# Weight staging, a PSUM bank for half-made weights, and one attention's exponentials and low parts moved between engines

## The chip, the cores and the metric

The kernel runs on one core of a Trainium2 chip. The metric is the device time of one execution in microseconds, the median of several runs. TensorE is called PE here, VectorE DVE, ScalarE ACT, GpSimd POOL and SyncE SP.

## The reference

A windowed attention is followed by two feed-forward networks on its output. Batch 4, 8 heads, 576 positions, head size 64; 2304 tokens, model width 512, inner width 2048.

```python
scores = scale * np.matmul(q, k.transpose(0, 1, 3, 2))
rel = pos[:, None] - pos[None, :]
mask_plain = (rel >= 0) & (rel < window)                                  # heads 0 to 3
mask_dil = (rel >= 0) & (rel < window * dilation) & (rel % dilation == 0)  # heads 4 to 7
scores = np.where(masks[None, :, :, :], scores, -1000000000.0)
attn = np.exp(scores - np.max(scores, axis=-1, keepdims=True))
attn = attn / (np.sum(attn, axis=-1, keepdims=True) + 1e-09)
x = np.matmul(attn, v)                  # then 2304 x 512
h = x @ w_in                            # first network
x = (np.maximum(h, 0.0) + alpha * np.minimum(h, 0.0)) @ w_out
h = x @ w_in2                           # second network
g = np.where(h >= 1, h, np.where(h <= -1, 0.0, (h + 1) ** 2 / 4.0))
out = g @ w_out2
```

## The kernel before

**The networks.** Activations stand in SBUF as X, 512 features on 4 x 128 partitions, 2304 tokens in the free dimension. Each network goes over five token tiles (512 wide, one of 256), and each tile over 16 slots, one for each 128 of the inner width: 160 slots in all. A product of fp32 numbers is made of three matmuls on a high and a low part of each operand. So `f_h` (L316) issues 12 matmuls of 512 columns into one bank of `ps_h`, which has two banks, and `f_y` (L355) issues 12 into the four banks of y. Between them `f_g` (L330) applies the nonlinearity: in the first network ACT makes relu(−h) into g (L339), the DVE makes h + alpha' g in place in the PSUM bank (L341), ACT copies that to gh (L347), and `f_cut` has the DVE make gl = h_ps − gh (L353), the last reader of the bank. PE's order is `f_h` of slot k, then `f_y` of slot k − 2. The low parts of the weights, wil (L288) and wol (L313), are made by POOL from a high part that ACT copied (L287, L312).

**The weights.** They arrive as 64-bit numbers. A weight piece (128 x 512) is loaded by SP into a staging buffer st (L248, 512 KB). Three operations of the DVE turn it into fp32: L276, L277 and L271. The first two are a mask and a shift of the upper word into wf or wo, each later one reads st and the half-made piece, both in SBUF. `conv(k)` issues k such operations; 5 or 6 come in each slot of tile 0, two of them ahead of L341 and one ahead of gl. There are five staging buffers for the first five pieces, three of which exist only at the beginning; later pieces have two. `more()` issues a load whenever a piece is done. In tile 4 and the next one the second network's weights are made in the same way.

**The attention.** It comes in 24 groups of 3 x 128 query rows, six for each batch. The six of batch 0 run at the beginning, with banks of their own; those of batches 1 to 3 are threaded through the first three tiles. There are two attention points in each slot, one after `f_h` and one after `f_y`, and a new group starts at every fifth point: `start` (scores, maximum, exponentials), then `a_turn` three points later (transposes, a copy to pT), `a_values` after five, `a_out` after eight (`STAGES`, L56). Each takes a bank of `ps_a`, which has two buffers used in turn. In batch 1 the mask is added on PE (L122), the maximum is read from PSUM (L136), and six exponentials of ACT read the scores from PSUM with the maximum as a bias (L143). Slots 0 and 1 have their `f_h` issued ahead of the slot loop (lines 466 to 485), so that between the start of group 7 and `f_h` of slot 2 PE has attention work alone.

**Order.** The kernel is scheduled by hand: each engine executes in the order in which the code issues, and waits at the first instruction that isn't ready. SP's queue is in order too. alpha and most of the mask are loaded from POOL's queue (L399, L400).

Of the kernel before, what the change touches and what calls it, by code (L numbers as in the profile page):

```python
# [10 lines left out]
F32 = mybir.dt.float32  # L11
# [11 lines left out]
P = 128  # L23
# [15 lines left out]
QK = KW + QW  # L39

NE = 8
EST = (2, 3, 4)
SCALE = 1.0 / math.sqrt(D)
NEG = -1.0e30
TILES = (
# [7 lines left out]
EARLY = (5, 6)  # L53
BEFORE = ((2, 1), (1, 3))

STAGES = (3, 5, 8)  # L56


def _subs(sb):
# [12 lines left out]
def attention_then_two_ffns(ctx: ExitStack, tc: tile.TileContext, a0, aqk, av, w1i, w1o, w2i, w2o, alpha, masks, ident, out):  # L72
# [6 lines left out]
    s_p = ctx.enter_context(tc.tile_pool(name="s_p", bufs=1))  # L79
    st_p = ctx.enter_context(tc.tile_pool(name="st_p", bufs=3))  # L80
    ps_h = ctx.enter_context(tc.tile_pool(name="ps_h", bufs=2, space=bass.MemoryType.PSUM))
    ps_a = ctx.enter_context(tc.tile_pool(name="ps_a", bufs=2, space=bass.MemoryType.PSUM))

    X = [const.tile([P, NT], F32, name=f"X{c}") for c in range(NC)]
    al = const.tile([P, NF], F32, name="al")
# [157 lines left out]

    def w_load(ph, f, part):
        w = ((w1i, w1o), (w2i, w2o))[ph][part]
        own = ph == 0 and pieces(0).index((ph, f, part)) in EST
        st = (sp if own else cv_p).tile([P, DM, 2], I32, tag="sx" if own else "st", name="st", bufs=len(EST) if own else 2)
        nc.sync.dma_start(st.rearrange("p a b -> p (a b)"), w[f].bitcast(I32))  # L248
        cv[ph, f, part] = st

    def w_make(ph, f, part):


        st = cv.pop((ph, f, part))
        top, low = st[:, :, 1], st[:, :, 0]
        if part:
            wf = w_pool(f).tile([P, DM], F32, tag=f"o{f}", name="wo")
            wo[ph, f] = wf
        else:
            hi = w_pool(f).tile([P, DM], F32R, tag=f"ih{f}", name="wih")  # L260
            lo = w_pool(f).tile([P, DM], F32R, tag=f"il{f}", name="wil")
            if ph == 0 and f in (1, 3):

                wf = sp.tile([P, DM], F32, tag="wx", name="wf")
            else:
                wf = cv_p.tile([P, DM], F32, tag="wf", name="wf", bufs=1)
            wt[ph, f] = (hi, lo)
        wi = wf.bitcast(I32)

        def last():  # L270
            nc.vector.scalar_tensor_tensor(wi, low, 29, wi, ALU.logical_shift_right, ALU.bitwise_or)  # L271
            if not part:
                cut.append((wf, hi, lo))

        return [
            lambda: nc.vector.tensor_scalar(wi, top, 0x07FFFFFF, 3, ALU.bitwise_and, ALU.logical_shift_left),  # L276
            lambda: nc.vector.scalar_tensor_tensor(wi, top, -0x40000000, wi, ALU.bitwise_and, ALU.bitwise_or),  # L277
            last,
        ]

# [22 lines left out]
    def wo_split(n, f):  # L303
        wf = wo[n[0], f]
        if (n, f) == slots[-1]:

            hi = cv_p.tile([P, DM], F32R, tag="wf", name="woh", bufs=1)
            lo = cv_p.tile([P, DM], F32R, tag="st", name="wol")
# [21 lines left out]
    def f_g(n, f, between):  # L330
        ph, t = n
        w = TILES[ph][t][1]
        ps = ht.pop((n, f))[:, :w]
        t = g_p.tile([P, TW], F32, tag="g", name="g", bufs=1)[:, :w]
        hi = g_p.tile([P, TW], F32R, tag="gh", name="gh")[:, :w]
        lo = g_p.tile([P, TW], F32R, tag="gl", name="gl")[:, :w]
        if ph == 0:

            nc.scalar.activation(t, ps, AF.Relu, scale=-1.0)  # L339
            between()  # L340
            nc.vector.scalar_tensor_tensor(ps, t, al[:, f:f + 1], ps, ALU.mult, ALU.add)  # L341
        else:
            nc.vector.tensor_scalar(t, ps, 1.0, -1.0, ALU.min, ALU.max)  # L343
            nc.scalar.activation(t, t, AF.Square, bias=half, scale=0.5)  # L344
            between()
            nc.vector.tensor_tensor(ps, ps, t, ALU.max)  # L346
        nc.scalar.activation(hi, ps, AF.Copy)  # L347
        gt[n, f] = (hi, lo)
        return ps

    def f_cut(n, f, ps):
        hi, lo = gt[n, f]
        nc.vector.tensor_tensor(lo, ps, hi.bitcast(F32), ALU.subtract)  # L353
# [33 lines left out]
    with tc.manual_schedule(), ExitStack() as late:  # L387
# [8 lines left out]
        warm = sp.tile([P, TW], BF16, tag="warm", name="warm")  # L396
        nc.scalar.dma_start(idt, ident)
        nc.scalar.dma_start(mask[:, :2 * GS], masks[:, :2 * GS])
        nc.gpsimd.dma_start(al, alpha)  # L399
        nc.gpsimd.dma_start(mask[:, 2 * GS:], masks[:, 2 * GS:])  # L400
        nc.vector.memset(warm, 0.0)
        nc.vector.memset(half, 0.5)
        pend_l = pieces(0)
# [2 lines left out]
        for i in range(NGB):  # L406
            a_load_qk(i)
            a_load_v(i)
            if i < 2 + len(EST):
                w_load(*pend_l.pop(0))  # L410
        nc.scalar.activation(half, half, AF.Exp, scale=0.0)
        nc.scalar.activation(half, half, AF.Copy, scale=0.5)
        for i in range(2):
# [84 lines left out]
        def attention_point():  # L498
# [4 lines left out]
                nxt += 1  # L503
            for i in list(at):
                k = point - at[i]
                if k == STAGES[0]:
                    a_turn(i, ps_a, "a")
                elif k == STAGES[1]:
                    a_values(i, ps_a, "a")
# [140 lines left out]
```

## Time and profile before

| | |
|---|---|
| median of 3 runs | 903.1 us (902.39 to 905.37) |
| the profiled execution | 902.28 us, of which the span is 900.5 us |
| PE busy | 875.4 us, 97% |
| DVE busy | 498.9 us, 55% |
| ACT busy | 372.3 us, 41% |
| POOL busy | 267.0 us, 30% |
| mean granted clock of PE | 0.981 of full |

A time in the trace counts from the start of the span. The busy shares are averages over stages with different limits, so the stretches are to be read one by one: the attention of batch 0 up to about 42 us, tile 0 with the making of the first network's weights up to about 146 us, tiles 1 to 3 up to 400 us, tile 4 and the first tile of the second network up to about 560 us, with weights again, and then matmuls alone.

### The profile page before, as it was taken

The page shows a single profiled execution, that of the slowest core. Times are in us where ns is not written, and L with a number is a line of the kernel's source. Part 1 is how long each engine was busy: PE and PEld are TensorE (multiplying, and loading weights), DVE is VectorE, ACT ScalarE, POOL GpSimd, SP SyncE. Part 2 cuts the span into 40 slices and gives each one's busy share as a digit, 9 for nine tenths or more (in the row PEclk, how much of TensorE's full clock was granted, in tenths as well). Part 3 has the DMA queues.
Part 4 walks back from the last instruction along what each step waited for, and adds up shares of the span by engine and source line. Part 5 has one row for each costly group of instructions (what it writes and reads, how often), then busy time and mean ns, then how long its engine had stood idle before and what let it go on. Part 6 is the DMA issues. An engine that isn't in the chain of part 4 may idle for free.

```text
span 900.5 us, 13858 instructions
## 1 busy us (share of the span) xinstructions
PE 875.4 (97%) x5470; PEld 720.6 (80%) x5470; DVE 498.9 (55%) x785; ACT 372.3 (41%) x745; POOL 267.0 (30%) x208
## 2 busy tenths in 40 slices
PE   7879899999999999999999999999999999999998
PEld 4568677888888888998888877888888888888898
DVE  6779897433353333346998896543354335433443
ACT  3434344534345334444334443433343334333454
POOL 3323331221212122444443343222222222222243
PEclk6789999999999999999999999999999999999999
DMA  9477463112112200001443331010001000100100
GB/s 360 140 197 211 138 189 106 38 41 71 38 41 71 65 1 1 1 2 47 138 133 104 118 125 39 1 47 1 0 1 48 1 0 1 47 1 0 44 5 24
DMA packets 24640, 59.34 MB, mean 66 GB/s; under 512 B 2752, under 2 KB 10448, under 8 KB 24576
## 3 DMA queue, kind: packets, MB, share of 16 engines
q1 hardware_dynamic: 24192, 58.09, 20.9%
q8 instruction: 43, 0.70, 0.3%
q14 instruction: 21, 0.17, 0.1%
q0 software_dynamic: 96, 0.20, 0.1%
q10 hardware_dynamic: 288, 0.16, 0.1%
HBM read 53.73 MB, written 4.72 MB: 65 GB/s over the span
## 4 chain that ended last, share of the span: by engine, by line
PE 81%; DVE 10%; DMA 4%; ACT 2%; issue 2%; SPq 0%; ACTq 0%; DVEq 0%
PE h_ps L326 13%; PE y L365 13%; PE y L367 13%; PE y L366 13%; PE h_ps L328 13%; PE h_ps L327 13%; DMA st<-w1o 2%; DVE wo L277 1%; DVE wo L271 1%; DVE gl L353 1%; DMA st<-w1i 1%; PE s_ps L129 1%; DVE wf L277 1%; PE t_ps L191 1%; PE o_ps L202 1%
## 5 line engine op out<-in xcount | busy, mean ns | idle before, releaser
L313 POOL TENSOR_TENSOR wol<-wo,woh 128x512 fp32r<-128x512 f32 x160 | 213.7, 1336 | 513.3 <-ACT woh L312 509.2
L326 PE MATMUL h_ps<-xh,wil 128*128 128x512 f32 (+1 forms) x640 | 242.5, 379 | 8.9 <-DVE gl L353 8.8
L365 PE MATMUL y<-gh,wol 128*128 128x512 f32 (+1 forms) x640 | 238.9, 373 | 0.6 <-POOL wol L313 0.6
L328 PE MATMUL h_ps<-xh,wih 128*128 128x512 f32 (+1 forms) x640 | 238.3, 372 | 0.0
L327 PE MATMUL h_ps<-xl,wih 128*128 128x512 f32 (+1 forms) x640 | 237.4, 371 | 0.0
L367 PE MATMUL y<-gl,woh 128*128 128x512 f32 (+1 forms) x640 | 236.7, 370 | 0.0
L366 PE MATMUL y<-gh,woh 128*128 128x512 f32 (+1 forms) x640 | 235.9, 369 | 0.0
L347 ACT ACTIVATE gh<-h_ps 128x512 fp32r<-128x512 f32 (+1 forms) x160 | 88.9, 556 | 212.5 <-PE y L366 97.5
L353 DVE TENSOR_TENSOR gl<-h_ps,gh 128x512 fp32r<-128x512 f32 (+1 forms) x160 | 102.0, 638 | 120.4 <-ACT gh L347 111.4
L326 PEld LDWEIGHTS h_ps<-xh,wil 128*128 128x128 f32 x640 | 121.2, 189 | 34.7 <-DVE gl L353 13.1
L328 PEld LDWEIGHTS h_ps<-xh,wih 128*128 128x128 f32 x640 | 121.2, 189 | 22.9
L365 PEld LDWEIGHTS y<-gh,wol 128*128 128x128 f32 x640 | 120.6, 188 | 22.8 <-issue 1.6
L327 PEld LDWEIGHTS h_ps<-xl,wih 128*128 128x128 f32 x640 | 121.4, 190 | 21.1 <-DVE xl L300 0.5
L367 PEld LDWEIGHTS y<-gl,woh 128*128 128x128 f32 x640 | 120.4, 188 | 21.9
L366 PEld LDWEIGHTS y<-gh,woh 128*128 128x128 f32 x640 | 120.5, 188 | 20.7
L344 ACT ACTIVATE g<-g,half 128x512 f32<-128x512 f32 (+1 forms) x80 | 54.5, 681 | 147.2 <-DVE g L343 147.0
L312 ACT ACTIVATE woh<-wo 128x512 fp32r<-128x512 f32 x160 | 99.6, 623 | 0.0
L341 DVE SCALAR_TENSOR_TENSOR h_ps<-g,al,h_ps 128x512 f32<-128x512 f32 (+1 forms) x80 | 55.9, 699 | 76.5 <-ACT g L339 75.9
L343 DVE TENSOR_SCALAR g<-h_ps 128x512 f32<-128x512 f32 (+1 forms) x80 | 50.8, 635 | 67.1 <-PE h_ps L328 66.8
L346 DVE TENSOR_TENSOR h_ps<-h_ps,g 128x512 f32<-128x512 f32 (+1 forms) x80 | 51.7, 646 | 60.5 <-ACT g L344 60.5
L288 POOL TENSOR_TENSOR wil<-wf,wih 128x512 fp32r<-128x512 f32 x32 | 44.6, 1394 | 110.4 <-ACT wih L287 106.0
L339 ACT ACTIVATE g<-h_ps 128x512 f32<-128x512 f32 (+1 forms) x80 | 44.2, 553 | 28.9 <-PE h_ps L328 28.8
(60 smaller groups left out, 513.8 us busy)
## 6 DMA issues: line engine op xcount, KB each, us to landing
st<-w1i SPq DMA_DIRECT2D x16, 512.0 KB, 4.1
st<-w1o SPq DMA_DIRECT2D x16, 512.0 KB, 3.8
st<-w2i SPq DMA_DIRECT2D x16, 512.0 KB, 3.2
st<-w2o SPq DMA_DIRECT2D x16, 512.0 KB, 3.3
qk<-aqk SPq DMA_DIRECT2D x36, 208.0 KB, 4.2
vz<-av SPq DMA_DIRECT2D x36, 195.0 KB, 4.2
out_t<-X SPq DMA_DIRECT2D x16, 256.0 KB, 2.0
e_in<-a SPq DMA_DIRECT2D x6, 416.0 KB, 8.8
```

The costliest lines, as they stand in the source:

```text
L312: nc.scalar.activation(hi, wf, AF.Copy)
L313: nc.gpsimd.tensor_tensor(lo, wf, hi.bitcast(F32), ALU.subtract)
L326: nc.tensor.matmul(ps[:, :w], wl[:, cs], xh[:, :w], start=(c == 0), stop=False)
L327: nc.tensor.matmul(ps[:, :w], wh[:, cs], xl[:, :w], start=False, stop=False)
L328: nc.tensor.matmul(ps[:, :w], wh[:, cs], xh[:, :w], start=False, stop=(c == NC - 1))
L341: nc.vector.scalar_tensor_tensor(ps, t, al[:, f:f + 1], ps, ALU.mult, ALU.add)
L344: nc.scalar.activation(t, t, AF.Square, bias=half, scale=0.5)
L347: nc.scalar.activation(hi, ps, AF.Copy)
L353: nc.vector.tensor_tensor(lo, ps, hi.bitcast(F32), ALU.subtract)
L365: nc.tensor.matmul(o, wl[:, cs], gh, start=(f == 0), stop=False)
L366: nc.tensor.matmul(o, wh[:, cs], gh, start=False, stop=False)
L367: nc.tensor.matmul(o, wh[:, cs], gl, start=False, stop=(f == NF - 1))
```

## The change

- All weight pieces go through five staging buffers `st` (NST) for the whole run; `more()` keeps up to five pieces loaded or in work. The room comes from a smaller descriptor scratch (`dynamic_dma_scratch_size`).
- From slot 0 on (`in_psum`) the first two operations of a piece write a PSUM bank, tag "w", and the third reads it and writes the piece to SBUF.
- `ps_a` has one buffer for tag "a" and one for tag "w" instead of two in turn. While pieces are being made, attention uses "a" alone; `bank()` alternates again when no pieces are left. In the first stage outputs use "w".
- Batch 1 subtracts the maximum with the DVE, from PSUM to SBUF, and one exponential of ACT follows.
- `STAGES` for batch 1 are 3, 4, 7 instead of 3, 5, 8.
- In the first network the DVE writes h + alpha' g to SBUF, into g, which has two buffers; gh and gl are made from there. In tile 0 POOL makes gl instead of the DVE.
- alpha and the rest of the mask are loaded from SP's queue behind the inputs of two groups.

```diff
-EST = (2, 3, 4)
+NST = 5
-STAGES = (3, 5, 8)
+STAGES = ((3, 4, 7), (3, 5, 8))
...
-    ps_a = ctx.enter_context(tc.tile_pool(name="ps_a", bufs=2, space=bass.MemoryType.PSUM))
+    ps_a = ctx.enter_context(tc.tile_pool(name="ps_a", bufs=1, space=bass.MemoryType.PSUM))
...
         src, s, mx = sc_t.pop(i)
+        if i < 2 * NGB:
+            nc.vector.tensor_tensor(s, src, mx[:, :, None].to_broadcast([P, 2 * GS, KEYS]), ALU.subtract)
+            nc.scalar.activation(s, s, AF.Exp, scale=SCALE)
+            s_t[i] = s
+            return
...
+        w0 = ps_a.tile([P, DM], F32, tag="w", name="w_ps").bitcast(I32) if in_psum else wi
...
-            nc.vector.scalar_tensor_tensor(wi, low, 29, wi, ALU.logical_shift_right, ALU.bitwise_or)
+            nc.vector.scalar_tensor_tensor(wi, low, 29, w0, ALU.logical_shift_right, ALU.bitwise_or)
...
-            lambda: nc.vector.tensor_scalar(wi, top, 0x07FFFFFF, 3, ALU.bitwise_and, ALU.logical_shift_left),
-            lambda: nc.vector.scalar_tensor_tensor(wi, top, -0x40000000, wi, ALU.bitwise_and, ALU.bitwise_or),
+            lambda: nc.vector.tensor_scalar(w0, top, 0x07FFFFFF, 3, ALU.bitwise_and, ALU.logical_shift_left),
+            lambda: nc.vector.scalar_tensor_tensor(w0, top, -0x40000000, w0, ALU.bitwise_and, ALU.bitwise_or),
...
-            nc.vector.scalar_tensor_tensor(ps, t, al[:, f:f + 1], ps, ALU.mult, ALU.add)
+            nc.vector.scalar_tensor_tensor(t, t, al[:, f:f + 1], ps, ALU.mult, ALU.add)
+            ps = t
...
-        nc.vector.tensor_tensor(lo, ps, hi.bitcast(F32), ALU.subtract)
+        (nc.gpsimd if n == order[0] else nc.vector).tensor_tensor(lo, ps, hi.bitcast(F32), ALU.subtract)
...
-        nc.gpsimd.dma_start(al, alpha)
-        nc.gpsimd.dma_start(mask[:, 2 * GS:], masks[:, 2 * GS:])
...
+            if i == 1:
+                nc.sync.dma_start(al, alpha)
+                nc.sync.dma_start(mask[:, 2 * GS:], masks[:, 2 * GS:])
...
-            while pend_l and sum(x[0] == 1 or pieces(0).index(x) not in EST for x in cv) < 2:
+            while pend_l and len(cv) + bool(todo) < NST:
                 w_load(*pend_l.pop(0))
...
+        def bank(i):
+
+            nonlocal turns
+            turns += not (todo or pend_w)
+            return "aw"[turns % 2]
```

PE's order where slots 0 and 1 begin. t_ps are the transposes of group 6, qk_88 the inputs of group 7, vz_89 the values of group 6, x_ps an output of the attention. Before:

```order
L191 MATMUL t_ps<-idt,s 128x128 x3
L122 LDWEIGHTS idt
L122 MATMUL s_ps<-mask,idt 32x384
...
L129 MATMUL s_ps<-qk_88 32x128 x12
L202 MATMUL o_ps<-vz_89,pT 32x130 x12
L326 MATMUL h_ps<-xh,wil 128x512
```

Now:

```order
L196 MATMUL t_ps<-idt,s 128x128 x3
L207 MATMUL o_ps<-vz_89,pT 32x130 x12
L122 LDWEIGHTS idt
L122 MATMUL s_ps<-mask,idt 32x384
...
L129 MATMUL s_ps<-qk_88 32x128 x12
L222 MATMUL x_ps<-idt,o 128x128 x3
L334 MATMUL h_ps<-xh,wil 128x512
```

The values of group 6 have moved ahead of the scores of group 7, and the output of group 6, which came after the twelve matmuls of slot 2, follows those scores directly.

The DVE's order at the same place, from the maximum of group 6 on. Before:

```order
L136 TENSOR_REDUCE mx<-s_ps 128x6
L141 TENSOR_SCALAR mx<-mx 128x6
L276 TENSOR_SCALAR wo<-st 128x512
L277 SCALAR_TENSOR_TENSOR wo<-st,wo 128x512
L271 SCALAR_TENSOR_TENSOR wo<-st,wo 128x512
L276 TENSOR_SCALAR wf<-st 128x512
L341 SCALAR_TENSOR_TENSOR h_ps<-g,al,h_ps 128x512
L277 SCALAR_TENSOR_TENSOR wf<-st,wf 128x512
L353 TENSOR_TENSOR gl<-h_ps,gh 128x512
L136 TENSOR_REDUCE mx<-s_ps 128x6
```

Now, from its subtraction on:

```order
L142 TENSOR_TENSOR s<-s_ps,mx 128x384
L284 TENSOR_SCALAR wo<-st 128x512
L285 SCALAR_TENSOR_TENSOR wo<-st,wo 128x512
L213 TENSOR_SCALAR rs<-o_ps 128x6
L214 RECIPROCAL rs<-rs 128x6
L215 TENSOR_TENSOR o<-o_ps,rs 128x384
L279 SCALAR_TENSOR_TENSOR wo<-st,wo 128x512
L284 TENSOR_SCALAR w_ps<-st 128x512
L349 SCALAR_TENSOR_TENSOR g<-g,al,h_ps 128x512
L285 SCALAR_TENSOR_TENSOR w_ps<-st,w_ps 128x512
L136 TENSOR_REDUCE mx<-s_ps 128x6
L142 TENSOR_TENSOR s<-s_ps,mx 128x384
```

The normalisation of group 6 (L213 to L215) now stands ahead of g of slot 0, gl is gone from this engine, and a subtraction stands behind each maximum.

SP's order of loads around the inputs of group 6 (qk_87) and of group 7 (qk_88). Before:

```order
L248 DMA st<-w1o 128x1024
L248 DMA st<-w1i 128x1024
L103 DMA qk_87<-aqk 64x832
L104 DMA qk_87<-aqk 64x832
L112 DMA vz_89<-av 64x3x260 x2
L248 DMA st<-w1o 128x1024
L248 DMA st<-w1i 128x1024
L103 DMA qk_88<-aqk 64x832
```

Now:

```order
L252 DMA st<-w1i 128x1024
L103 DMA qk_87<-aqk 64x832
L104 DMA qk_87<-aqk 64x832
L112 DMA vz_89<-av 64x3x260 x2
L252 DMA st<-w1o 128x1024
L252 DMA st<-w1i 128x1024
L252 DMA st<-w1o 128x1024
L103 DMA qk_88<-aqk 64x832
```

Two more pieces stand ahead of the first of these rows and one more between the inputs of the two groups; the piece next ahead of qk_88 waits in both for the DVE's last operation on an earlier piece.

## Rows read from the trace of the kernel before

**Rows 1.** Busy us of each engine by stretch, then clock, DMA share, GB/s

```profile
42.50:60.00 17.50, 11.37 (x89) 8.69 (x90) 12.06 (x20) 6.46 (x18) 4.77 (x4) 0.90 0.89 236
60.00:146.30 86.30, 81.60 (x572) 64.95 (x570) 79.02 (x114) 36.95 (x89) 30.57 (x22) 0.96 0.58 170
...
160.00:400.00 240.00, 240.00 (x1670) 202.07 (x1669) 89.44 (x169) 105.24 (x239) 59.81 (x46) 1.00 0.14 35
400.00:560.00 160.00, 158.52 (x712) 129.04 (x711) 134.81 (x180) 66.05 (x117) 63.85 (x47) 1.00 0.30 99
```

**Rows 2.** Waits of PE over the span: us in total, times, longest us

```profile
PE h_ps L326 <- DVE gl L353: 8.8, 8, 3.1
...
PE s_ps L129 <- DMA qk<-aqk: 2.9, 1, 2.9
...
PE y L365 <- POOL wol L313: 0.6, 1, 0.6
```

**Rows 3.** Groups of DVE instructions, 40 to 145 us: busy us, mean ns | idle before

```profile
L271 DVE SCALAR_TENSOR_TENSOR wo<-st,wo 128x512 int32<-128x512 int32 x14 | 16.3, 1162 | 0.3
L277 DVE SCALAR_TENSOR_TENSOR wo<-st,wo 128x512 int32<-128x512 int32 x14 | 14.8, 1054 | 0.3
L271 DVE SCALAR_TENSOR_TENSOR wf<-st,wf 128x512 int32<-128x512 int32 x12 | 10.5, 873 | 0.3
L341 DVE SCALAR_TENSOR_TENSOR h_ps<-g,al,h_ps 128x512 f32<-128x512 f32 x14 | 10.5, 748 | 0.0
L277 DVE SCALAR_TENSOR_TENSOR wf<-st,wf 128x512 int32<-128x512 int32 x12 | 10.4, 871 | 0.2
L353 DVE TENSOR_TENSOR gl<-h_ps,gh 128x512 fp32r<-128x512 f32 x13 | 9.0, 690 | 2.2 <-ACT gh L347 1.2
L276 DVE TENSOR_SCALAR wf<-st 128x512 int32<-128x512 int32 x11 | 7.9, 720 | 3.5 <-DMA st<-w1i 3.5
L276 DVE TENSOR_SCALAR wo<-st 128x512 int32<-128x512 int32 x14 | 7.0, 497 | 3.2 <-DMA st<-w1o 3.2
...
L136 DVE TENSOR_REDUCE mx<-s_ps 128x6 f32<-128x384 f32 x6 | 3.3, 550 | 0.9 <-PE s_ps L129 0.9
```

**Rows 4.** Timelines of DVE and POOL about 61 us: start, duration

```profile
60.75 0.69 DVE L277 SCALAR_TENSOR_TENSOR wo<-st,wo 128x512 int32<-128x512 int32 x1
61.47 1.67 DVE L271 SCALAR_TENSOR_TENSOR wo<-st,wo 128x512 int32<-128x512 int32 x1
...
61.12 1.47 POOL L288 TENSOR_TENSOR wil<-wf,wih 128x512 fp32r<-128x512 f32 x1 [3.27 <-ACT wih L287]
```

**Rows 5.** The largest group of POOL, 40 to 146 us

```profile
L313 POOL TENSOR_TENSOR wol<-wo,woh 128x512 fp32r<-128x512 f32 x13 | 19.2, 1474 | 24.4 <-ACT woh L312 20.3 <-DMA vz<-av 4.0
```

**Rows 6.** The DVE's subtraction of the maximum in batch 0, 5 to 40 us

```profile
L170 DVE TENSOR_TENSOR s<-s_ps,mx 128x384 f32<-128x384 f32 x6 | 3.3, 558 | 0.4
```

**Rows 7.** The DVE's tensor_scalar on PSUM in the second network, 400 to 560 us

```profile
L343 DVE TENSOR_SCALAR g<-h_ps 128x512 f32<-128x512 f32 x12 | 8.2, 682 | 1.0 <-PE h_ps L328 1.0
```

**Rows 8.** Timelines of PE and (one row) DVE; in brackets idle before and releaser

```profile
42.53 1.15 PE L191 MATMUL t_ps<-idt,s 128*128 128x128 f32 x3 [1.23 <-ACT s L143]
...
46.81 1.51 PE L129 MATMUL s_ps<-qk 128*32 128x128 f32 x24 [2.86 <-DMA qk<-aqk]
48.06 1.55 PE L202 MATMUL o_ps<-vz,pT 128*32 128x130 f32 x24
49.55 0.53 PE L326 MATMUL h_ps<-xh,wil 128*128 128x512 f32 x1
...
58.02 0.43 DVE L276 TENSOR_SCALAR wf<-st 128x512 int32<-128x512 int32 x1 [2.66 <-DMA st<-w1i]
...
59.10 0.50 PE L326 MATMUL h_ps<-xh,wil 128*128 128x512 f32 x1 [3.08 <-DVE gl L353]
...
65.25 0.50 PE L365 MATMUL y<-gh,wol 128*128 128x512 f32 x1
...
110.13 0.50 PE L326 MATMUL h_ps<-xh,wil 128*128 128x512 f32 x1 [1.85 <-DVE gl L353]
```

More of the change, by code (lines that the diff above doesn't have):

```diff
@@ L245, in w_load @@
         w = ((w1i, w1o), (w2i, w2o))[ph][part]
-        own = ph == 0 and pieces(0).index((ph, f, part)) in EST
-        st = (sp if own else cv_p).tile([P, DM, 2], I32, tag="sx" if own else "st", name="st", bufs=len(EST) if own else 2)
+        st = cv_p.tile([P, DM, 2], I32, tag="st", name="st", bufs=NST)
         nc.sync.dma_start(st.rearrange("p a b -> p (a b)"), w[f].bitcast(I32))
         cv[ph, f, part] = st
+    in_psum = False
     def w_make(ph, f, part):
@@ L307, in wo_split @@
             hi = cv_p.tile([P, DM], F32R, tag="wf", name="woh", bufs=1)
-            lo = cv_p.tile([P, DM], F32R, tag="st", name="wol")
+            lo = cv_p.tile([P, DM], F32R, tag="st", name="wol", bufs=NST)
         else:
@@ L333, in f_g @@
         ps = ht.pop((n, f))[:, :w]
-        t = g_p.tile([P, TW], F32, tag="g", name="g", bufs=1)[:, :w]
+        t = g_p.tile([P, TW], F32, tag="g", name="g")[:, :w]
         hi = g_p.tile([P, TW], F32R, tag="gh", name="gh")[:, :w]
@@ L408, in attention_then_two_ffns @@
             a_load_v(i)
-            if i < 2 + len(EST):
+            if i < NST:
                 w_load(*pend_l.pop(0))
+            if i == 1:
+                nc.sync.dma_start(al, alpha)
+                nc.sync.dma_start(mask[:, 2 * GS:], masks[:, 2 * GS:])
         nc.scalar.activation(half, half, AF.Exp, scale=0.0)
@@ L439, in conv @@
                         more()
+        def bank(i):
+            nonlocal turns
+            turns += not (todo or pend_w)
+            return "aw"[turns % 2]
+        turns = 0
         def start(i):
-            a_scores(i, ps_a, "a", i < 2 * NGB)
+            a_scores(i, ps_a, bank(i), i < 2 * NGB)
             a_load_qk(i + 2)
@@ L455, in attention_then_two_ffns @@
             if i >= 2:
-                a_out(i - 2, ps_a, "a")
+                a_out(i - 2, ps_a, "w")
             w_cut()
@@ L467, in attention_then_two_ffns @@
         a_turn(NGB - 1, ps_a, "a")
-        a_out(NGB - 2, ps_a, "a")
+        a_out(NGB - 2, ps_a, "w")
         f_h(n0, 1, (0,))
@@ L472, in attention_then_two_ffns @@
         f_h(n0, 1, (1,))
-        a_out(NGB - 1, ps_a, "a")
+        a_out(NGB - 1, ps_a, "w")
         f_h(n0, 0, (2,))
@@ L487, in attention_then_two_ffns @@
         first.close()
+        in_psum = True
         wl_p = late.enter_context(tc.tile_pool(name="wl_p", bufs=1))
@@ L505, in attention_point @@
                 k = point - at[i]
[L506 to L509, printed above, removed]
+                stages = STAGES[i >= 2 * NGB]
+                if k == stages[0]:
+                    a_turn(i, ps_a, bank(i))
+                elif k == stages[1]:
+                    a_values(i, ps_a, bank(i))
                     a_load_v(i + 2)
-                elif k == STAGES[2]:
-                    a_out(i, ps_a, "a")
+                elif k == stages[2]:
+                    a_out(i, ps_a, bank(i))
                     del at[i]
@@ L627 @@
     from concourse.bass_utils import run_bass_kernel_spmd
-    nc = bacc.Bacc("TRN2", target_bir_lowering=False, num_devices=1)
+    nc = bacc.Bacc("TRN2", target_bir_lowering=False, num_devices=1, dynamic_dma_scratch_size=1024)
     a0, aqk, av = _attention_layout(q, k, v)
```

## The prediction

> **What bounds the kernel now.** I read the stretches first, then the waits of TensorE, then the instructions of the engine that they name. The stretches [rows 1] say where something can be had at all: from 160 to 400 us PE is busy 240.00 of 240.00 us at full clock, so nothing that the change does there can bring time, it can only cost. What is open lies elsewhere: 17.50 − 11.37 = 6.1 us of idle PE from 42.5 to 60, 86.30 − 81.60 = 4.7 us from 60 to 146.3, 1.5 us from 400 to 560. The granted clock is 0.90 and 0.96 in the first two. PE is at either the full or the half level, so a mean of 0.96 over 86.3 us is 2 × 0.04 × 86.3 = 6.9 us at half, of which half, some 3.4 us, is lost; the drops follow the long waits, one the 3.08 us at 59.10, one the 1.85 us at 110.13 [rows 8].
>
> The waits [rows 2] name one cause for most of it: PE's first matmul into h_ps waits for the DVE's gl, 8.8 us in 8 places. h_ps has two banks and gl is the last reader of one. In both stretches the DVE is nearly full (79.02 of 86.30 us [rows 1]), so it sets the pace of the first token tile, and PE waits whenever it has fallen a slot behind. Why it is full stands in its groups [rows 3]: the three operations that make a weight piece take 0.43 us (L276 at 58.02, [rows 8]) or 0.69 us (L277 at 60.75, [rows 4]) when nothing runs on POOL, but on average 0.72 and 0.50 (L276, wf and wo), 0.87 and 1.05 (L277), 0.87 and 1.16 us (L271). [Rows 4] show the disturbance: POOL's wil runs from 61.12 to 62.59, and an L271 beside it takes 1.67 us. Operations with one operand in PSUM show none of it: L341 means 0.748 over 14, L353 0.690 over 13 [rows 3]. A second cause is the load: the DVE stood 2.66 us at 58.02 for a weight piece, and the 3.08 us of PE end just behind that [rows 8]. A third is PE's 2.86 us before 46.81, for the qk of group 7 [rows 2, 8].
>
> **The pieces in PSUM.** Of a piece's three operations none reads two SBUF operands any more. L276 gets its output in PSUM; the nearest row is L343, a tensor_scalar that reads PSUM, 0.682 [rows 7]; the other end is its present 0.497 [rows 3]. The other two I take at 0.69 (L353), at most 0.748 (L341). A piece costs 0.68 + 2 × 0.69 = 2.06 us (1.88 to 2.22) after 0.60 + 0.97 + 1.03 = 2.60 now (means over the wf and wo groups). That is 0.54 us (0.38 to 0.72) over 26 pieces, 14 us of DVE.
>
> [...]
>
> **gl on POOL in tile 0.** 0.69 us leave the DVE in each of 13 slots, 9.0 us. POOL takes 14 more operations of 1.474 us [rows 5], 20.6 us, on top of 4.77 + 30.57 us [rows 1]: 56 of 104, it has room. Behind gl in POOL's queue stands wol of the same slot, which y needs more than a slot later; its single wait was 0.6 us [rows 2]. The recurrence also changes: STT g now writes SBUF, so h_ps is free after it and no longer after gh and gl. The wait of 8.8 us then hangs on a result that comes at least 0.6 + 0.69 us sooner.
>
> **Exponentials from SBUF.** One subtraction of 0.558 us [rows 6] per group of batch 1 joins the DVE, 6 × 0.558 = 3.3 us; a tiny scaling goes, at nothing. ACT has one exponential for six. The bank is free after the subtraction.
>
> The DVE's sum from 42.5 to 146.3: 12.06 + 79.02 = 91.1 us, less 14 and 9.0, plus 3.3, is 71 of 103.8 us, 69% where it was 88%. It stops setting the pace.
>
> **One bank for the attention in tile 0.** ps_a had two buffers in turn; now every scores, transpose, values and output of a group uses the one bank "a" while pieces are made, and each must wait until the one before is read out. In steady slots about twelve matmuls of PE lie between two uses; the read-outs are 0.55 + 0.56 us (maximum and subtraction, [rows 3, 6]) or one copy. A DVE that is 69% full is there in time, so I cost this at nothing, with one exception. At the start slots 0 and 1 have no matmuls of their own: the scores of group 7 and the output of group 6 now follow each other directly, and the second waits for the first's subtraction. Step by step [rows 8]: transposes as before, to 43.7; copy, then values of group 6 at about 44.2 to 45.0, in the hole before the load of qk that lands at 46.8. That hides the 1.55 us which they took at 48.06. The DVE then has the norm (to 46.0), a piece operation (46.7), another (47.4), g (48.1), another (48.8), and only then maximum and subtraction, to 49.9. The output transposes come at 50.0 and h_ps of slot 2 at 50.5, where it was 49.55: 0.95 us later.
>
> **Five staging buffers.** Pieces are loaded up to five ahead, in the idle of the queue before 41 us, so the 2.66 us at 58.02 goes. The load of qk for group 7 still stands behind a piece that waits for the same DVE operation; 46.8 stays. From slot 2 to the first y of slot 1 it was 65.25 − 49.55 = 15.7 us; without the 3.08 us wait, without the 1.7 us of half clock behind it (half of the 3.4 us) and without the 0.33 us of output transposes that are now earlier, 10.6 us: 50.5 + 10.6 = 61.1, 4.1 us sooner. If the new idle before 50 brings a half clock of its own, 2.4 us. I take 3.4.
>
> **The moved loads.** alpha and the masks leave POOL's queue for SP's, 0.2 MB behind two groups' inputs. The same bytes went through the same engines before; nothing.
>
> **The sum.** Up to 65.25: 3.4 us (2.4 to 4.1). From there to 146.3: 4.7 us of waits and 1.7 us of clock could all go, 6.4; I take 5.5, since new small waits are likely, and 2 as the low end. From 400 to 560: 1.0 of the 1.5 us (0 to 1.5). Together 9.9 us (4.4 to 12.0). The profiled execution took 902.28 us, 0.8 under the median of 903.1, its span 900.5. 902.28 − 9.9 = 892.4; I say 892.5 for the median.
>
> **The rivals.** *The single bank makes PE wait (slower).* If the DVE stays behind by more than half a slot, each of the six groups of batch 1 meets a bank that is not read out, at its scores and again at its output. Two waits of 1.1 us each (the two read-out operations) are 2.2, and a wait like the 1.85 us at 110.13 [rows 8] brings 1.7 us of half clock besides, say in every second group: 6 × (2.2 + 0.85) = 18 us against the gain of 9.9, 902.28 + 8.4 or about 911 us. It decides from 9.9 / 6 = 1.65 us a group. For it speaks that the start has such a wait; against it the DVE's 69%. 0.08.
>
> *PE keeps most of its waits.* The operations on PSUM are still lengthened, or POOL, with gl ahead of wil and wol, becomes the late one: only the start's 2.4 us and about 2 us are left, 898 to 900 us. Against it speak L341 and L353, never long. 0.13.
>
> *The DVE is stretched elsewhere.* In tiles 1 to 4 gl stays on the DVE, but it now reads g and gh from SBUF, both. In tile 4 pieces of the second layer are made too, 4.5 operations a slot. With gl at 1.67 instead of 0.69 us [rows 4] a slot of the DVE is 4.5 × 0.69 + 0.75 + 1.67 = 5.5 us, just what a slot lasts on PE ((900.5 − 49.55) / 158 = 5.4 us). In a stretch where the DVE is busy 134.81 of 160 us already [rows 1] a tie can cost 0.2 us on each of 16 slots, 3 us: 895.5. 0.07. [...]
>
> *The start opens too.* If group 7's scores or the DVE's chain come sooner than I reckon, up to 4 us more of the hole from 41.3 to 50 close: 888. 0.08.
>
> **How the numbers follow.** The forecast keeps 0.64. A measurement of this kernel can tell about 0.3%, 2.7 us. Faster by more than that: 0.64 + 0.07 + 0.08 and 0.05 of the second rival, 0.84. Within it: the other 0.08 of that rival, 0.08. Slower: 0.08. The range takes the bounds of the sum, 890.3 to 897.9, the start's rival down to 888 and half of the second rival, up to 899.5; what lies outside is 0.08 slower, some 0.06 of the second rival and a few hundredths below.
>
> **What would show it.** DVE busy near 70% from 42.5 to 146, no L271 or L277 successor over 0.8 us while pieces go through w_ps; no wait of PE for g after 60 us; PE busy over 99% from 65 us on; tile 0 done at about 137 to 139 us where it was 146; the output of group 6 at about 50 us, with a wait for the DVE ahead of it. I am wrong if PE's waits name the DVE's s or o on bank "a" again and again, if POOL's wol or gl stands ahead of y, or if the clock shows half in more places than one behind 50 us.

## The result, and the profile after

The changed kernel takes 891.31 us (890.96 to 891.61, 4 runs) beside 903.81 us of the kernel before on the same chip: a ratio of 0.9858, 95% interval 0.9846 to 0.9871. Its profiled execution has a span of 889.8 us, 10.7 less than before. In a second set, run as `after_again`, it takes 890.7 us, ratio 0.9863 (0.9841 to 0.9885). The medians lie 12.5 us apart; the profiled execution of the kernel before was one of its quicker ones (902.28 us), so the two traces show 10.7 us of that.

The stretches of the changed kernel, as in [rows 1] (PE, PEld, DVE, ACT, POOL busy, clock, DMA share, GB/s):

```profile
42.50:60.00 17.50, 12.78 (x112) 9.55 (x113) 15.96 (x28) 8.74 (x16) 9.30 (x8) 0.80 1.00 279
60.00:146.30 86.30, 86.30 (x625) 67.79 (x624) 62.69 (x103) 37.09 (x73) 45.40 (x36) 1.00 0.49 145
...
400.00:560.00 160.00, 159.93 (x703) 130.65 (x702) 116.34 (x178) 66.39 (x113) 58.47 (x47) 1.00 0.27 89
```

From 60 to 146.3 us PE never stands, at full clock. The DVE fell from 79.02 to 62.69 us there, in part because the stretch now takes in about 8 us of tile 1, which asks less of it. From 42.5 to 138.3 us, about as much work as from 42.5 to 146.3 before, it is busy for 73.21 us, where it was 91.1. Between 42.5 and 60 PE is still idle for 4.7 us and the clock fell to 0.80. The waits of PE over the span, to be held against [rows 2] (us in total, times, longest):

```profile
PE t_ps L196 <- ACT s L143: 1.6, 1, 1.6
PE x_ps L222 <- DVE s L142: 1.4, 1, 1.4
...
PE s_ps L122 <- DVE o L215: 1.1, 1, 1.1
...
PE s_ps L129 <- DMA qk<-aqk: 0.7, 1, 0.7
...
PE h_ps L334 <- DVE gl L362: 0.3, 1, 0.3
```

Of the 8.8 us for gl 0.3 are left, in the second network's last tile. What remains stands in the start of tile 0. The groups of the DVE, 40 to 137 us, against [rows 3]:

```profile
L285 DVE SCALAR_TENSOR_TENSOR w_ps<-st,w_ps 128x512 int32<-128x512 int32 x24 | 16.6, 694 | 0.5
L284 DVE TENSOR_SCALAR w_ps<-st 128x512 int32<-128x512 int32 x24 | 16.6, 692 | 0.6
L349 DVE SCALAR_TENSOR_TENSOR g<-g,al,h_ps 128x512 f32<-128x512 f32 x15 | 11.1, 743 | 6.1 <-ACT g L347 6.1
L279 DVE SCALAR_TENSOR_TENSOR wo<-st,w_ps 128x512 int32<-128x512 int32 x13 | 8.9, 685 | 0.3
L279 DVE SCALAR_TENSOR_TENSOR wf<-st,w_ps 128x512 int32<-128x512 int32 x11 | 7.5, 684 | 1.3 <-POOL wil L296 0.7
```

A piece costs 0.694 + 0.692 + 0.685 = 2.07 us, and none of its operations is lengthened. The start, on PE, against [rows 8]:

```profile
43.50 0.55 PE L196 MATMUL t_ps<-idt,s 128*128 128x128 f32 x3 [1.55 <-ACT s L143]
44.63 0.87 PE L207 MATMUL o_ps<-vz,pT 128*32 128x130 f32 x24 [0.58 <-ACT pT L198]
46.60 0.35 PE L122 MATMUL s_ps<-mask,idt 128*32 128x384 bf16 x4 [1.10 <-DVE o L215]
47.63 1.51 PE L129 MATMUL s_ps<-qk 128*32 128x128 f32 x24 [0.68 <-DMA qk<-aqk]
50.49 0.88 PE L222 MATMUL x_ps<-idt,o 128*128 128x128 f32 x3 [1.35 <-DVE s L142]
51.02 0.78 PE L334 MATMUL h_ps<-xh,wil 128*128 128x512 f32 x1
51.59 0.63 PE L335 MATMUL h_ps<-xl,wih 128*128 128x512 f32 x1
52.02 0.63 PE L336 MATMUL h_ps<-xh,wih 128*128 128x512 f32 x1
...
63.21 0.50 PE L374 MATMUL y<-gh,wol 128*128 128x512 f32 x1
```

Values of group 6 run in the hole, the output of group 6 waits 1.35 us for the subtraction of group 7, and the first matmuls of slot 2 come 0.43 us apart (51.59 and 52.02), at the half level: the granted clock there is 0.50, from 47.5 to 54.0 us. At 1.00, from 54.5 us on, they come 0.23 us apart (54.62 and 54.85).

Where the time went, by the same events of both profiled executions (us from the span's start; y counts as read out when ACT's first copy of it begins):

| event | before | after | gained so far |
|---|---|---|---|
| scores of group 6 begin | 38.20 | 38.85 | −0.65 |
| `f_h` of slot 2 | 49.55 | 51.02 | −1.47 |
| first y of slot 1 | 65.25 | 63.21 | 2.04 |
| y of tile 0 read out | 162.7 | 154.7 | 8.0 |
| y of tile 4 read out | 498.5 | 490.2 | 8.3 |
| y of the second network's first tile read out | 589.3 | 578.8 | 10.5 |
| end of span | 900.5 | 889.8 | 10.7 |

### The profile page after: what moved, and what is told of

It is laid out like the page before. It is cut to its first block, busy times and chain, and to the rows that moved or that the text cites. A ratio compares the mean times of both kernels' runs of the same rounds, so it can differ in the third digit from the quotient of the medians.

```text
span 889.8 us, 13837 instructions
## 1 busy us (share of the span) xinstructions
PE 871.0 (98%) x5470; PEld 717.8 (81%) x5470; DVE 461.6 (52%) x769; ACT 371.6 (42%) x715; POOL 277.0 (31%) x222
## 2 busy tenths in 40 slices
DMA packets 24832, 59.34 MB, mean 67 GB/s; under 512 B 2880, under 2 KB 10688, under 8 KB 24768
## 4 chain that ended last, share of the span: by engine, by line
PE 95%; DMA 2%; DVE 1%; ACT 1%; issue 1%; SPq 0%; ACTq 0%
PE h_ps L334 15%; PE y L374 15%; PE y L376 15%; PE h_ps L336 15%; PE y L375 15%; PE h_ps L335 15%; DMA e_in<-a 2%; PE s_ps L129 2%; PE o_ps L207 1%; PE x_ps L222 1%; PE t_ps L196 1%; DMA qk<-aqk 1%; PE o_ps L189 0%; PE s_ps L165 0%; ACT pT L198 0%
## 5 line engine op out<-in xcount | busy, mean ns | idle before, releaser
L321 POOL TENSOR_TENSOR wol<-wo,woh 128x512 fp32r<-128x512 f32 x160 | 207.8, 1299 | 481.6 <-ACT woh L320 481.6
L374 PEld LDWEIGHTS y<-gh,wol 128*128 128x128 f32 x640 | 120.6, 188 | 21.7 <-issue 1.8
L353 ACT ACTIVATE g<-g,half 128x512 f32<-128x512 f32 (+1 forms) x80 | 54.5, 681 | 147.4 <-DVE g L352 147.2
L349 DVE SCALAR_TENSOR_TENSOR g<-g,al,h_ps 128x512 f32<-128x512 f32 (+1 forms) x80 | 55.3, 692 | 86.7 <-ACT g L347 86.5
L356 ACT ACTIVATE gh<-g 128x512 fp32r<-128x512 f32 (+1 forms) x80 | 47.2, 589 | 120.5 <-PE y L375 80.1
L362 DVE TENSOR_TENSOR gl<-h_ps,gh 128x512 fp32r<-128x512 f32 (+1 forms) x80 | 51.0, 637 | 56.6 <-ACT gh L356 56.6
L362 DVE TENSOR_TENSOR gl<-g,gh 128x512 fp32r<-128x512 f32 (+1 forms) x64 | 40.0, 626 | 70.7 <-ACT gh L356 62.8
L356 ACT ACTIVATE gh<-h_ps 128x512 fp32r<-128x512 f32 (+1 forms) x80 | 44.4, 555 | 71.4 <-PE y L375 48.2
```

The lines of the kernel that those rows point to most:

```text
L349: nc.vector.scalar_tensor_tensor(t, t, al[:, f:f + 1], ps, ALU.mult, ALU.add)
L362: (nc.gpsimd if n == order[0] else nc.vector).tensor_tensor(lo, ps, hi.bitcast(F32), ALU.subtract)
L374: nc.tensor.matmul(o, wl[:, cs], gh, start=(f == 0), stop=False)
```

## The experiments

**Theory:** in tile 0 the DVE set the pace, chiefly by piece operations on two SBUF operands that POOL's operations lengthen (an L271 of the kernel before took 1.67 us at 61.47 beside wil and 0.69 at 66.98 with POOL idle); with these gone it has room, and then the rest follows. **Rivals:** the earlier release of h_ps carries the gain; the staging carries it; the single bank costs nothing or much. Kernels whose label begins with u_ undo one part of the change (u_psum_g two), those with o_ put one part into the kernel before (o_psum_st two), those with c_ go on from the change.

**u_psum**, pieces in SBUF again:

```diff
-        w0 = ps_a.tile([P, DM], F32, tag="w", name="w_ps").bitcast(I32) if in_psum else wi
+        w0 = ps_a.tile([P, DM], F32, tag="w", name="w_ps").bitcast(I32) if False else wi
```

> The changed kernel (891.3 us) with weight pieces made in SBUF again, as before; all else of the change stays. Theory (the DVE set the pace in tile 0, and pieces in PSUM took the most off it): L279, L284 and L285 are stretched again to about 2.6 to 3.0 us a piece, since POOL now has three operations a slot; the DVE goes from 62.7 to 75 to 82 of 86.3 us in tile 0, PE waits come back in part, for g or for bank a: 893 to 896 us. Rival (what counted was that h_ps no longer waits for gl; the DVE's load alone costs nothing): within 0.7 us of 891.3, PE busy 86 of 86.3 us from 60 us on.

Measured: 904.83 us, ratio to before 1.0016 (1.0003 to 1.0029). The whole gain is gone, and the time is 9 us over the theory's upper end. Groups of its DVE, 40 to 146 us, and its stretch:

```profile
L279 DVE SCALAR_TENSOR_TENSOR wo<-st,wo 128x512 int32<-128x512 int32 x14 | 16.1, 1148 | 0.3
L285 DVE SCALAR_TENSOR_TENSOR wo<-st,wo 128x512 int32<-128x512 int32 x14 | 15.4, 1101 | 0.3
L284 DVE TENSOR_SCALAR wo<-st 128x512 int32<-128x512 int32 x14 | 12.3, 877 | 0.0
...
60.00:146.30 86.30, 80.53 (x568) 62.43 (x568) 76.36 (x101) 32.84 (x66) 48.26 (x34) 0.98 0.51 150
```

A wo piece takes 3.13 us. The DVE is not quite full (76.36 of 86.30), yet PE stands 5.8 us there. Where, show ACT and PE about 76 us:

```profile
75.19 0.63 ACT L295 ACTIVATE wih<-wf 128x512 fp32r<-128x512 f32 x1 [3.19 <-DVE wf L279]
75.73 0.80 ACT L240 ACTIVATE X<-x_ps 128x192 f32<-128x192 f32 x2
...
76.59 0.55 PE L196 MATMUL t_ps<-idt,s 128*128 128x128 f32 x3 [2.87 <-ACT X L240]
```

ACT stands in order behind a piece that the DVE finishes late, so the read-out of bank a behind it is late, and PE waits for the bank. This is the slower rival of the prediction in another part's absence. Of the 12.4 us by which this execution's span is longer than the change's, 9.2 are lost by the time y of tile 0 is read out and 2.3 in the second network's first tile.

**u_g**, g and gl as before:

```diff
-            nc.vector.scalar_tensor_tensor(t, t, al[:, f:f + 1], ps, ALU.mult, ALU.add)
-            ps = t
+            nc.vector.scalar_tensor_tensor(ps, t, al[:, f:f + 1], ps, ALU.mult, ALU.add)
...
-        (nc.gpsimd if n == order[0] else nc.vector).tensor_tensor(lo, ps, hi.bitcast(F32), ALU.subtract)
+        nc.vector.tensor_tensor(lo, ps, hi.bitcast(F32), ALU.subtract)
```

> The changed kernel with g back in PSUM and gl back on the DVE, reading PSUM, so that h_ps is again free only after gl. Theory (DVE pace): the DVE rises by 14 x 0.69 = 9.7 us to 72 of 86.3 us in tile 0, still not full, so at most 1 us of waits for gl come back: 891 to 892.5 us. Rival (the order of release counted): the waits of PE for gl come back nearly whole, 5 to 7 us with the half clock: 896 to 898 us.

Measured: 892.38 us (890.18 to 893.12), ratio 0.9877 (0.9845 to 0.9908), not to be told from the whole change. Its stretch:

```profile
60.00:146.30 86.30, 86.30 (x624) 67.78 (x623) 70.87 (x119) 37.77 (x75) 28.42 (x22) 1.00 0.49 146
```

The DVE takes the 8 us back and PE loses nothing. With pieces in PSUM the earlier release of h_ps brings nothing that can be told; that rival falls.

**u_psum_g**, the edits of u_psum and u_g together:

> The changed kernel with both undone: pieces in SBUF, g in PSUM and gl on the DVE. Staging, one bank, single exponential and stages stay. Theory (what made u_psum slow was POOL's third operation a slot lengthening SBUF operations): without gl on POOL the pieces are back at about 2.6 us, DVE about 88% full, PE's waits for gl as before but none for loads: 897 to 901 us. Rival (SBUF pieces alone are enough to lose everything): 903 to 906 us as u_psum.

Measured: 899.09 us, ratio 0.9941 (0.9918 to 0.9963), in the theory's range, but not by its waits. Waits of its PE over the span:

```profile
PE s_ps L122 <- DVE o L215: 2.5, 3, 1.1
PE t_ps L196 <- ACT X L240: 1.6, 2, 1.1
PE h_ps L334 <- DVE gl L361: 1.6, 4, 0.6
...
PE o_ps L207 <- ACT pT L198: 1.5, 2, 0.9
```

All four waits for gl come after 400 us. From 60 to 146.3 us PE is idle for 4.2 us, most of it three waits on bank a (0.8, 1.1 and 0.9 us), for the normalisation and for two copies of ACT: once the rest of the change is in, a late DVE shows there. With gl on the DVE in both, pieces in SBUF cost 899.09 − 892.38 = 6.7 us (u_g), about half of the gain, not the whole. With pieces in SBUF, gl on POOL makes things worse by 904.83 − 899.09 = 5.7 us: it takes 0.69 us a slot off the DVE and lengthens its SBUF operations (a wo piece from 2.77 to 3.13 us), so that the DVE is as busy from 60 to 146.3 us as without (76.36 and 76.86 us).

**o_g**, g in SBUF and gl on POOL put into the kernel before (the diff of u_g the other way round):

> The kernel before (903.8 us) with one part of the change: h + alpha' g goes to SBUF, g has two buffers, and gl is made by POOL in tile 0. Pieces stay in SBUF, two staging buffers. Theory (DVE pace): 9.0 us leave the DVE but two more POOL operations in three slots lengthen its piece operations; half of the waits after 60 us go, the 3.1 us at 59 shrinks by the 0.4 to 0.7 us of gl only, as the load is late: 899 to 902 us. Rival (the release of h_ps counted): the 8.8 us of waits for gl go, with 3 us of half clock: 893 to 896 us.

Measured: 904.85 us, ratio 1.0018 (1.0004 to 1.0032): both expectations missed, and the rival by 9 us. Its mechanism was there all the same. Waits of PE:

```profile
PE y L366 <- POOL wol L313: 4.9, 4, 2.1
...
PE s_ps L122 <- ACT X L235: 2.6, 2, 2.4
PE h_ps L326 <- DVE gl L354: 1.8, 5, 0.6
```

The waits for gl in tile 0, 7.2 of the 8.8 us, are gone (what is left comes after 400 us). But POOL, with gl between wil and wol, is now the late one, as the prediction's second rival had it, and a bank of the attention too is read out late. That part alone brings nothing, as u_psum against u_psum_g says too.

**u_stage**, at most two pieces ahead:

```diff
-            while pend_l and len(cv) + bool(todo) < NST:
+            while pend_l and len(cv) + bool(todo) < 2:
```

> The changed kernel with the rule of loading at most two pieces ahead, the first five as they are. Theory (the load was a second cause, the 2.66 us at 58.02): the DVE waits for loads again between 45 and 60 us and by 1 us here and there later; with a DVE that is 73% busy most of it is absorbed: 891.5 to 894 us. Rival (the staging carries the gain): 896 us or more.

Measured: 898.16 us, ratio 0.9944 (0.9928 to 0.996): 6.9 us more than the change: over what the theory allowed, and in the rival's range, though not the whole gain. SP's queue about 42 us (issues) and a group of the DVE:

```profile
42.59 0.60 SPq L104 DMA_DIRECT2D qk<-aqk  x1
48.29 1.20 SPq L112 DMA_DIRECT2D vz<-av  x2
49.60 0.54 SPq L252 DMA_DIRECT2D st<-w1o  x1
...
L284 DVE TENSOR_SCALAR w_ps<-st 128x512 int32<-128x512 int32 x24 | 16.6, 692 | 8.5 <-DMA st<-w1o 4.6 <-DMA st<-w1i 3.6
```

SP stands 5 us with the values of a later group, whose buffer PE has not yet read, and all pieces stand behind that. The DVE waits 8.2 us for loads, in two places more than 1.3 us just where the start hangs on it. `f_h` of slot 2 comes at 53.47 and the first y of slot 1 at 67.25, 4.0 us later than in the change; its scores of group 6 were 2.3 us late already (41.16). This execution's span is 5.5 us longer than the change's; 2.3 us of that stand before those scores, where executions of one kernel differ as much (`after_again`), and 3.2 us behind them.

**o_psum**, the PSUM bank alone in the kernel before, with the one bank for attention that it needs:

```diff
-    ps_a = ctx.enter_context(tc.tile_pool(name="ps_a", bufs=2, space=bass.MemoryType.PSUM))
+    ps_a = ctx.enter_context(tc.tile_pool(name="ps_a", bufs=1, space=bass.MemoryType.PSUM))
...
+        w0 = ps_a.tile([P, DM], F32, tag="w", name="w_ps").bitcast(I32) if in_psum else wi
...
+            return "aw"[turns % 2]
```

> The kernel before (903.4 us) with the PSUM part of the change alone: pieces half-made in a PSUM bank, one bank each for attention and pieces. gl stays on the DVE and reads PSUM, two staging buffers, six exponentials from PSUM. Theory (unstretched piece operations free the DVE; the load is the next limit): DVE 79.0 to 69 of 86.3 us in tile 0; PE waits for gl shrink to those behind a late load; the waits for the load stay, as u_stage had them: 896 to 900 us. Rival (single bank with slow read-out, six exponentials holding it): new waits of PE on bank a, 902 to 906 us.

Measured: 923.61 us, ratio 1.021 (1.0184 to 1.0236). Both expectations missed widely. Waits of its PE:

```profile
PE o_ps L202 <- ACT s L143: 13.2, 5, 3.3
PE t_ps L191 <- ACT X L235: 10.3, 5, 6.4
```

With stages 3, 5, 8 a group's values come at the same attention point as the next group's scores, and its transposes at the same point as the output of the group before; both pairs now use one bank. The values wait for six exponentials, the transposes for the copy to X. From 60 to 146.3 us PE is busy 65.93 us, the clock is 0.90.

**o_psum_st**, the same with the stages of the change for batch 1:

```diff
-STAGES = (3, 5, 8)
+STAGES = ((3, 4, 7), (3, 5, 8))
```

> The kernel before with pieces in PSUM, one bank (o_psum, 923.6 us) and the stages 3, 4, 7 for batch 1. Theory (its loss was the single bank with uses back to back): the 13 us of waits of values for exponentials and the 10 us of transposes for the copy to X go nearly whole, 897 to 903 us; two staging buffers still cost some. Rival (SP's queue or the six exponentials were the cause): 912 us or more.

Measured: 901.93 us, ratio 0.9978 (0.9964 to 0.9991), 21.7 us less than o_psum. The order of the uses was the cause. What this kernel lacks of the change costs 6.9 (u_stage), 3.3 (u_exp) and 1.1 us (u_g) when it is undone singly, together about 11, and it is 10.6 us slower than the change: little is left for the moved loads, which no run undoes.

**u_stages**, the change with the stages of before:

```diff
-STAGES = ((3, 4, 7), (3, 5, 8))
+STAGES = ((3, 5, 8), (3, 5, 8))
```

> The changed kernel with batch 1's stages 3, 5, 8 as before. With these, values of a group follow the next group's scores at the same attention point, and transposes follow an output at the same point, without matmuls of the networks between. Theory (the single bank is bearable only because the stages put about twelve matmuls between two uses of it): at each of the groups PE waits for the subtraction ahead of the values, about 1.3 us, and for the copy to X ahead of the transposes, 0.8 to 1.3 us; with half clocks 8 to 18 us more, 899 to 909 us. Rival (a DVE and an ACT with room read the bank out in time anyway): 891 to 893.5 us.

Measured: 907.52 us, ratio 1.0041 (1.0027 to 1.0054), 16.8 us over `after_again` beside it. Its waits, and PE about 57 us:

```profile
PE t_ps L196 <- ACT X L240: 7.0, 5, 3.5
PE o_ps L207 <- issue: 6.6, 5, 1.3
...
56.74 0.49 PE L222 MATMUL x_ps<-idt,o 128*128 128x128 f32 x3
60.72 0.55 PE L196 MATMUL t_ps<-idt,s 128*128 128x128 f32 x3 [3.49 <-ACT X L240]
```

Five times transposes stand behind an output, five times values behind scores. For the second the profile names no releaser, but the values begin each of the five times 0.10 us after a subtraction of the DVE (L142) ends, for example at 70.64 after 69.98 + 0.56: they wait for the bank that the subtraction of the next group's scores reads.

**u_exp**, six exponentials from PSUM in batch 1:

```diff
-        if i < 2 * NGB:
+        if i < 0:
```

> The changed kernel with batch 1's six exponentials from PSUM again, no subtraction on the DVE; bank a is then held until the sixth has read it. Theory (with a DVE that has room the bank is free in time either way, but at the start the output of group 6 waits for the bank): the wait of 1.35 us ahead of it grows by about 1 us, elsewhere nothing: 891.5 to 893.5 us. Rival (the single bank depends on the quick read-out everywhere): waits on bank a in most of the six groups, 895 us or more.

Measured: 894.58 us, ratio 0.9888 (0.9863 to 0.9914), 3.3 us over the change (the intervals of the two ratios overlap a little). The theory's place is right and its size too small; from 60 to 146.3 us PE is busy 86.30 of 86.30 us here too. The start, and its stretch:

```profile
52.05 0.90 PE L222 MATMUL x_ps<-idt,o 128*128 128x128 f32 x3 [3.54 <-ACT s L148]
...
42.50:60.00 17.50, 11.81 (x83) 9.00 (x84) 13.93 (x23) 8.28 (x20) 8.01 (x7) 0.61 1.01 271
```

The wait for the bank grew from 1.35 to 3.54 us, and the half clock behind it lasts longer: the granted clock of the stretch is 0.61, where the change had 0.80.

**c_both**, the output of group 6 and the scores of group 7 in banks of y, the inputs of group 7 loaded earlier:

```diff
+            if i == NGB + 1:
+                a_scores(i, ps_y, "y2", True)
...
+                    if i == NGB:
+                        a_out(i, ps_y, "y3")
...
+                a_load_qk(NGB + 1)
+                a_load_v(NGB + 1)
```

> The changed kernel, and besides: the output of group 6 and the scores of group 7 use two banks of y, which are idle until the first y, and the inputs of group 7 are loaded two groups earlier. Theory (the start loses 1.10 + 0.68 + 1.35 us of waits and a half clock behind them, on the bank and on the load of qk): f_h of slot 2 begins at 48.5 to 49.5 instead of 51.0 us, 1.6 to 4 us less in all: 887.3 to 889.7 us. Rival (the start hangs on the DVE's order, on g of slot 0 above all): within 0.7 us of 891.3.

Measured: 890.14 us (887.94 to 890.8), ratio 0.9835 (0.9806 to 0.9864). `f_h` of slot 2 began at 48.71 and the first y of slot 1 at 61.64, 1.6 us before the change's. The start came as the theory had it, the time lies between the two expectations, and against 891.31 and 890.7 us of the change it stays unclear.

**c_start**, besides that the maximum and subtraction of group 6 ahead of the piece operations:

```diff
-        conv(3)
-        w_cut()
         start(NGB)
+        conv(3)
+        w_cut()
         f_h(n0, 1, (2,))
-        conv(2)
...
-EARLY = (5, 6)
+EARLY = (7, 6)
```

> The kernel of c_both (890.1 us), and besides the DVE takes maximum and subtraction of group 6 ahead of the five piece operations that stood about it; the two that are left over come in slot 0. Theory (the start hangs on the DVE's order): the transposes of group 6 lose their wait of 1.6 us, g of slot 0 comes about 2 us sooner, f_h of slot 2 begins at 46.5 to 47.5 us: 887.5 to 889 us. Rival (a wait or a half clock elsewhere takes its place): within 0.7 us of 890.1.

Measured: 891.37 us, ratio 0.9862 (0.9848 to 0.9877): no gain over c_both. `f_h` of slot 2 came at 47.49 as expected, and a new wait took its place, with one for g ahead of it:

```profile
PE y L374 <- ACT X L240: 2.4, 1, 2.4
PE h_ps L334 <- DVE g L349: 1.4, 1, 1.4
```

The first y must wait, at its fourth bank, until the output is read out of the bank that was lent; ACT comes to that copy late. The rival's mechanism holds; the time is 1.2 us over c_both, more than the 0.7 that it allowed.

**after_again**, the change once more:

> The changed kernel once more, beside the next three on one chip: 890.5 to 892.0 us by every theory.

Measured: 890.7 us (889.35 to 893.06).

## Why the prediction was right, point by point

The sum came out near for better and worse reasons. Its three terms were 3.4, 5.5 and 1.0 us; the traces show 2.0, 6.0 and 2.2, and 0.5 elsewhere: the misses are of both signs, and that the total (9.9 forecast, 10.7 in the traces, 12.5 by the medians) is so close is in part luck. Two parts had no term of their own, the stages and the staging beyond one wait, and undoing either loses most of the gain or all of it.

- **What bounds.** Right in the main: with the piece operations at 2.07 us PE has no wait from 60 to 146 us, and u_psum, which takes the PSUM bank away, loses everything. But part of that loss is gl on POOL lengthening SBUF pieces (a wo piece 3.13 us in u_psum, 2.77 in u_psum_g); with gl on the DVE in both, the bank is worth 6.7 us (u_psum_g against u_g). Nor is it enough alone: with its stages, but without staging, it gives 901.93 us (o_psum_st). The DVE's sum was forecast at 71 us up to 146.3; 73.21 us were measured for about the same work, up to 138.3.
- **Readings of the rows.** Two were off, and one point was passed over. The DVE was nearly full in the second stretch only; in the first it was busy 12.06 of 17.50 us. L277 at 60.75 is not undisturbed, for POOL's wil starts within it, at 61.12; L277 at 58.96, between two operations of POOL, took 0.68 us and gives the same value. And an operation needn't read two SBUF operands to be lengthened: L276 reads st alone, took 0.42 us in most places, and 1.53 us beside POOL's wol:

```profile
96.08 1.53 DVE L276 TENSOR_SCALAR wf<-st 128x512 int32<-128x512 int32 x1
...
95.57 1.76 POOL L313 TENSOR_TENSOR wol<-wo,woh 128x512 fp32r<-128x512 f32 x1
```

  With its output in PSUM (L284) none of 24 took over 0.698 us. That PE is at the full or the half level holds in the trace of the kernel before: of its quarter microseconds up to 160 us 499 show a granted clock of 1.00, 133 of 0.50, and the 8 others are those in which it goes from one to the other. From 60 to 146.3 us the half level stands up to 63.3 and from 111.1 to 114.5.
- **The pieces in PSUM.** 2.06 us a piece were forecast, 2.07 measured. The operation L284 went from 0.43 us undisturbed (one piece made in SBUF at 39.9 us) to 0.692 with its output in PSUM, as the 0.68 taken from L343 had it. It reads st in both; the output alone differs.
- **gl on POOL.** Of the 9 us that it was to take off the DVE 8.2 came (62.69 us against 70.87 in u_g, 60 to 146.3), but they are worth no time that can be told. The step that the wait "then hangs on a result that comes at least 0.6 + 0.69 us sooner" explained a gain that needed no such cause (u_g); in the kernel before it does remove the waits for gl, and waits for POOL take their place (o_g). The sum held because the DVE's load was no term of it; only the waits were.
- **One bank, cost at nothing.** Right for the change as a whole, and for the reason given: twelve matmuls between two uses. But the new stages got no term of their own. They are what puts the matmuls there: without them 16.8 us are lost (u_stages). The slower rival was the right mechanism, with the wrong condition: it doesn't need a late DVE, the order of the uses is enough (a late DVE does it too, u_psum). It priced 18 us for it.
- **The start.** 3.4 us (2.4 to 4.1) forecast, 2.04 measured, below the range. 0.65 us of the shortfall stood before the scores of group 6, and `after_again` began its scores of group 6 at 36.78 against 38.85 us here, so that much varies between executions. From those scores on the gain is 27.05 − 24.36 = 2.7 us. `f_h` of slot 2 was forecast at 50.5 and came at 51.02, with the half clock behind it (0.50 up to 54.0 us), which the low end had and my value left out.
- **From there to 146 us.** 5.5 forecast, 8.0 − 2.04 = 6.0 measured: nearly all of the 6.4 us there were.
- **400 to 560 us.** 1.0 forecast, 2.2 measured, in the second network's first tile (90.8 us before, 88.6 after, by the table). Pieces in PSUM carry this: by the same events every run that has them takes 88.5 to 88.6 us for that tile, and every run with pieces in SBUF 90.8 to 91.1 (u_psum, u_psum_g, o_g). PE's idle time accounts for 1.4 us of it; why its busy time also fell, by 0.8 us, is not settled.
- **Staging.** Counted as the 2.66 us wait; undone it costs 6.9 us. In the trace of u_stage SP stands 5 us with attention loads and the pieces behind them come late; that accounts for some 3.2 us, and the rest stays open.
- **The moved loads.** Put at nothing; no run undoes them alone. Both traces have 59.34 MB over the 16 DMA engines; of these 0.20 MB, 0.1% of the engines' time, left POOL's queue, and SP's went from 20.9 to 21.0%.
- **gl from SBUF in tiles 1 to 4.** That rival fell. The group of tile 4 in the changed kernel:

```profile
L362 DVE TENSOR_TENSOR gl<-g,gh 128x512 fp32r<-128x512 f32 x16 | 11.1, 692 | 12.4 <-ACT gh L356 12.4
```

  It isn't lengthened, and of all 64 in tiles 1 to 4 the longest took 0.695 us. Of one slot, its place on the DVE and POOL's next operation:

```profile
421.18 0.69 DVE L362 TENSOR_TENSOR gl<-g,gh 128x512 fp32r<-128x512 f32 x1 [0.17 <-ACT gh L356]
...
421.75 1.30 POOL L321 TENSOR_TENSOR wol<-wo,woh 128x512 fp32r<-128x512 f32 x1 [1.40 <-ACT woh L320]
```

  gl starts when ACT has made gh, and POOL's wol waits for woh, which ACT makes next. The order keeps them apart, but for the last 0.12 us (421.75 against 421.18 + 0.69), so a lengthening like that of L271 beside wil (1.67 us, [rows 4]) has hardly an occasion here.

## What to carry to other kernels

An operation that another engine lengthens can cost more than its own time, for engines in order behind it are late too: in u_psum the DVE was busy for 76.36 of 86.30 us, yet ACT stood 3.19 us behind one piece and PE 2.87 us behind ACT. Here it paid to move one operand out of SBUF (6.7 us, u_psum_g against u_g) before moving work from the DVE to POOL: the other way round brought nothing (o_g) or cost 5.7 us (u_psum against u_psum_g). When a buffer goes from two to one, count what stands between two uses in each engine's order, not how busy its readers are: with the stages 3, 4, 7 for 3, 5, 8 a kernel with one bank went from 923.61 to 901.93 us (o_psum, o_psum_st). Parts of a change can depend on each other: here the PSUM bank alone lost 2.1%, while undoing the bank, the staging or the stages singly cost 7 to 17 us of a gain of 12.5.

## What the runs showed of the hardware that I had not expected

The DVE's SBUF operations took longer in the run in which POOL had more to do: a wo piece took 2.77 us in u_psum_g and 3.13 in u_psum, with POOL busy for 31.42 and 48.26 us from 60 to 146.3; of its three operations L284 and L285 grew (0.635 to 0.877 and 0.927 to 1.101 us), L279 didn't (1.212 and 1.148). POOL's own wol took 1.474 us before, 1.620 in u_psum and 1.304 in the changed kernel, where the DVE's piece operations have an operand in PSUM. And the time to the scores of group 6 differs by up to 2.1 us between executions of one kernel (36.78 and 38.85 us, `after_again` and the change).
